# Attention and highway layer on one core: PSUM as eight planned banks, a searched order of issue, and x of the last two duos transposed by DMA

## The chip, the cores and the metric

One NeuronCore of a Trainium2 chip runs the whole program. The metric is the device time in microseconds of one execution, the median of several. The profile's span, from the first to the last instruction, is some 2 us shorter than that time (183.9 against 185.97 for the kernel before).

## The reference

Sliding-window attention with a linear bias (window 128), then a highway layer. Batch 8, 8 heads, 576 positions, head size 64; the layer has 4608 rows of 512.

```python
scores = scale * q @ k.T - slope[h] * |i - j|      # only 0 <= i - j < 128
attn   = softmax(scores); x = attn @ v             # [8, 576, 8 * 64] -> [4608, 512]
H = max(x @ w_h, 0); T = sigmoid(x @ w_t + b_t)
out = T * H + (1 - T) * x
```

## The kernel before

Two batches make a "duo"; duo 0 is cut into stages a, b, c, d, the others into A and B (3B is stage B of duo 3, and its blocks are "3B blocks"). For each stage TensorE (PE) transposes q and k, makes scores, ScalarE (ACT) takes the exponential, VectorE (DVE) multiplies by a mask, PE makes PV, and DVE divides into x. For each block of 128 rows of x, PE transposes x, ScalarE copies it out as xt, and PE computes h (x @ w_h) and z (x @ w_t); this part after the attention is called the FFN. DVE, ScalarE and GpSimd (POOL) combine, and the sync queue (SP) stores. Every instruction belongs to a small piece called a node; a list of nodes gives the order in which all engines' queues are filled. Each engine has a queue of its own, filled in that order.

```python
    psp = ctx.enter_context(tc.tile_pool(name="ps", bufs=BUFS["ps"], space=PSUM))   # bufs 4
    def ps_tile(dt=F32):
        return psp.tile([P, 2, 512 if dt == F32 else 1024], dt, name="ps")          # two banks each
    ...
    def load_v(m, c):                                   # on the gpsimd queue
        n = min(P, S - c * P)
        nc.gpsimd.dma_start(out=VA[m % 2][0:n, c, :, :, 0:D]..., in_=v[...]...)
    def c_ones(i):                                      # column D of each head's slot in v: the row sums
        nc.vector.memset(VA[i][:, :, :, :, D : D + 1], 1.0)
    ...
    def f_xd(m, kind, gi):                              # there, but unused before: DMA_X = ()
        for i in range(n):
            nc.sync.dma_start_transpose(out=xt[:, i], in_=x[:, i, :])
    def f_st(m, kind, gi):                              # four stores a block (two for the short block)
        ...
        for t in range(4):
            nc.sync.dma_start(out=dst[t], in_=ot[32 * t : 32 * t + 32, 0 : len(bs), :])
    ...
    order, end = plan(SHIFT, LOOKS)                     # list scheduling by priorities
    with tc.manual_schedule():
        for t, key in order:
            nodes[key][3]()
```

The softmax here doesn't subtract the row's maximum and nothing guards it: scores larger than these inputs give would overflow.

## Time and profile before

| what | value |
|---|---|
| time, median before the prediction | 185.97 us |
| span of the profile | 183.9 us |
| PE busy | 155.0 us (84%) |
| DVE busy | 141.6 us (77%) |
| last matmul to the end of the span | 6.9 us |

Rows of PE overlap in the profile (four h matmuls are 1.04 us as a row of the timeline and 0.86 us as a piece of the chain of waits), so the pieces of the chain are taken as the price of a group.

### The profile page before, as it was taken

The numbers are of one execution on the slowest core, as the hardware profiler recorded it, in microseconds if no ns is written. First come the engines' busy times: TensorE is split into PE (matmuls) and PEld (weight loads), VectorE is DVE, ScalarE is ACT, GpSimd is POOL, SyncE is SP. The second block draws the span as 40 slices with busy tenths as digits, with TensorE's granted clock in tenths as the row PEclk, the third lists the DMA queues.
The fourth block names the chain that finished last, engine by engine and source line by source line (L and its number), as shares of the span: only waits on it lengthen the run. The fifth ranks groups of instructions, "written<-read, shape, count | busy, mean of one in ns | idle before, by whom it ended". The sixth has DMA issues, their size and how long they took to land.

```text
span 183.9 us, 5244 instructions
## 1 busy us (share of the span) xinstructions
PE 155.0 (84%) x2132; PEld 93.9 (51%) x2132; DVE 141.6 (77%) x253; ACT 127.8 (69%) x178; POOL 121.5 (66%) x132
## 2 busy tenths in 40 slices
PE   0286886779999957997999999999998999999950
PEld 0264655655564524675554565665444666555510
DVE  5339885699999893697688999799899788866770
ACT  2558595753889953879779889786998888445510
POOL 7994123979999945984269953544487787667540
PEclk9999999999999996999999999999999999999995
DMA  4999999999999999999997994142212322243543
GB/s 157 225 187 198 200 199 176 138 132 92 127 207 228 210 200 205 135 187 225 208 135 96 178 159 90 45 103 61 57 45 74 93 66 74 74 103 99 137 128 94
DMA packets 70167, 25.50 MB, mean 139 GB/s; under 512 B 48128, under 2 KB 65024, under 8 KB 70144
## 3 DMA queue, kind: packets, MB, share of 16 engines
q0 software_dynamic: 62832, 14.68, 113.6%
q1 hardware_dynamic: 7312, 10.49, 21.3%
q8 instruction: 16, 0.26, 0.6%
q14 instruction: 7, 0.06, 0.1%
HBM read 30.41 MB, written 9.44 MB: 217 GB/s over the span
## 4 chain that ended last, share of the span: by engine, by line
PE 38%; DMA 26%; DVE 16%; POOL 7%; ACT 5%; issue 3%; SPq 1%; POOLq 0%; DVEq 0%; ACTq 0%
DMA kl<-in_k_dram 24%; PE ps L460 10%; PE ps L443 9%; DVE pt L363 6%; PE ps L386 6%; PE ps L270 5%; PE ps L328 5%; DVE x L403 4%; POOL ot L484 3%; DMA out_dram<-ot 3%; ACT pt L344 2%; PE ps L462 2%; DVE uu L450 2%; POOL ql L110 2%; PE ps L426 2%
## 5 line engine op out<-in xcount | busy, mean ns | idle before, releaser
L344 ACT ACTIVATE pt<-ps,bias 128x1024 bf16<-128x1024 f32 (+1 forms) x80 | 73.4, 951 | 9.1 <-PE ps L328 8.4
L484 POOL TENSOR_TENSOR ot<-uu,x 128x512 f32<-128x512 bf16 x35 | 49.7, 1421 | 30.4 <-DVE uu L478 28.9
L363 DVE TENSOR_TENSOR pt<-pt,mk 128x2048 bf16<-128x2048 bf16 (+1 forms) x40 | 47.8, 1210 | 0.7 <-ACT pt L344 0.5
L460 PE MATMUL ps<-wT,xt 128*128 128x512 bf16 x144 | 38.0, 387 | 1.2 <-DVE uu L450 0.7
L443 PE MATMUL ps<-wH,xt 128*128 128x512 bf16 x144 | 37.2, 380 | 0.6 <-DVE uu L450 0.3
L122 POOL DMA_DIRECT2D va<-in_v_dram x20 | 22.2, 1117 | 14.3 <-DMA kl<-in_k_dram 8.2
L450 DVE SCALAR_TENSOR_TENSOR uu<-ps,x 128x512 bf16<-128x512 f32 x36 | 24.8, 688 | 7.7 <-PE ps L443 7.3
L468 ACT ACTIVATE tt<-ps 128x512 f16<-128x512 f32 x36 | 21.5, 598 | 11.6 <-PE ps L462 11.1
L328 PE MATMUL ps<-qt,kt 64*128 64x256 bf16 (+2 forms) x384 | 27.2, 254 | 1.8 <-DVE kt L295 1.4
L473 POOL TENSOR_SCALAR tt<-tt 128x512 f16<-128x512 f16 x32 | 23.1, 722 | 5.6 <-ACT tt L468 5.5
L435 ACT COPY xt<-ps 128x512 bf16<-128x512 bf16 x36 | 21.0, 586 | 8.1 <-PE ps L426 7.2
L403 DVE TENSOR_TENSOR x<-ps,rd 128x256 bf16<-128x256 f32 (+3 forms) x40 | 25.5, 637 | 1.4
L386 PEld LDWEIGHTS <-pt 128*128 128x128 bf16 (+1 forms) x576 | 21.2, 101 | 8.0 <-issue 1.8
L386 PE MATMUL ps<-va,pt 128*128 128x65 bf16 (+1 forms) x576 | 24.1, 196 | 1.3 <-ACT kt L295 0.4
L295 ACT COPY kt<-ps 128x1024 bf16<-128x1024 bf16 x13 | 13.1, 1012 | 14.4 <-PE ps L270 8.4
L289 DVE COPY qt<-ps 128x1024 bf16<-128x1024 bf16 x16 | 10.9, 687 | 14.2 <-PE ps L270 10.9
L478 DVE TENSOR_TENSOR uu<-uu,tt 128x512 bf16<-128x512 bf16 x36 | 16.6, 462 | 4.9 <-POOL tt L473 2.9
L270 PE MATMUL ps<-ident,ql 128*64 128x128 bf16 (+1 forms) x320 | 13.3, 242 | 8.3 <-DMA ql<-in_q_dram 7.5
L443 PEld LDWEIGHTS <-xt 128*128 128x128 bf16 x144 | 12.1, 97 | 14.4 <-issue 2.8
L460 PEld LDWEIGHTS <-xt 128*128 128x128 bf16 x144 | 12.4, 99 | 13.7 <-issue 3.9
L328 PEld LDWEIGHTS <-kt 64*128 64x128 bf16 x384 | 12.8, 97 | 12.6 <-issue 7.0
L270 PE MATMUL ps<-ident,kl 128*64 128x128 bf16 (+1 forms) x320 | 12.8, 242 | 6.6 <-DMA kl<-in_k_dram 5.6
(46 smaller groups left out, 127.9 us busy)
## 6 DMA issues: line engine op xcount, KB each, us to landing
out_dram<-ot SPq DMA_DIRECT2D x128, 64.0 KB, 1.8
va<-in_v_dram POOLq DMA_DIRECT2D x16, 256.0 KB, 10.8
ql<-in_q_dram POOLq DMA_DIRECT2D x3, 1024.0 KB, 14.6
kl<-in_k_dram POOLq DMA_DIRECT2D x3, 1024.0 KB, 18.8
ql<-in_moe_w_h_dram SPq DMA_DIRECT2D x1, 1024.0 KB, 5.8
out_dram<-ot SPq DMA_DIRECT2D x8, 128.0 KB, 2.4
ql<-in_q_dram POOLq DMA_DIRECT2D x4, 128.0 KB, 5.8
kl<-in_k_dram POOLq DMA_DIRECT2D x4, 128.0 KB, 5.9
```

What stands on the lines that cost most here:

```text
L122: nc.gpsimd.dma_start(out=VA[m % 2][0:n, c, :, :, 0:D].rearrange("s r h d -> s (r h) d"), in_=v[2 * m : 2 * m + 2, :, c * P : c * P + n, : ...
L270: nc.tensor.transpose(out=pt[r * D : (r + 1) * D, c : c + n], in_=L[ps, r, nh * hs + hl, t * D : (t + 1) * D], identity=ident[ps, ps],)
L328: nc.tensor.matmul(out=sc[:, r, o + off : o + off + w_], lhsT=KT[i][rows, h, j * P : (j + 1) * P], rhs=rhs, start=not add, stop=not add or ...
L344: nc.scalar.activation(out=PT[m, home, h // 2][:, h % 2, :, c0 : c0 + W], in_=SC[m, kind, h][:, :, o : o + W], func=ACTF.Exp, bias=BIAS[:, ...
L363: nc.vector.tensor_tensor(out=o, in0=o, in1=mk.to_broadcast([P, 2, rep, W]), op=ALU.mult,)
L386: nc.tensor.matmul(out=av[rows, hl, n * (D + 1) : (n + 1) * (D + 1)], lhsT=pt[:, hl, r, off : off + (D if narrow else P)], rhs=va[:, j, r, ...
L403: nc.vector.tensor_tensor(out=x.rearrange("p b (h d) -> p h b d", h=2), in0=av[:, :, :, 0:D], in1=rd[:, :, 0:nb].to_broadcast([P, 2, nb, D ...
L443: nc.tensor.matmul(out=AH[m, kind, gi][:, i, :], lhsT=XT[m, kind, gi][:, i, c, :], rhs=wH[:, c, :], start=c == 0, stop=c == NCK - 1)
L450: nc.vector.scalar_tensor_tensor(out=uu[:, 0:n, :], in0=AH[m, kind, gi][:, 0:n, :], scalar=0.0, in1=x, op0=ALU.max, op1=ALU.subtract,)
L460: nc.tensor.matmul(out=az, lhsT=XT[m, kind, gi][:, i, c, :], rhs=wT[:, c, :], start=c == 0, stop=False)
L473: eng.tensor_scalar(out=tt, in0=tt, scalar1=0.5, scalar2=0.5, op0=ALU.mult, op1=ALU.add)
L484: eng.tensor_tensor(out=ot[:, 0:n, :], in0=UU.pop((m, kind, gi))[:, 0:n, :], in1=x, op=ALU.add)
```

## The change

Its intent: give each PSUM user only the banks it needs, replace the list scheduler by an order and a bank plan found by a search, and take the x transposes of the last two duos (18 blocks) off PE and ScalarE. The core of the diff (cuts marked "..."):

```diff
-    DMA_X = ()
+    DMA_X = (6, 7, 8, 9)
-    psp = ctx.enter_context(tc.tile_pool(name="ps", bufs=BUFS["ps"], space=PSUM))
+    psp = ctx.enter_context(tc.tile_pool(name="ps", bufs=1, space=PSUM))
+    PSB = psp.tile([P, 8, 512], F32, name="ps")
+    def ps_tile(nb, dt=F32):
+        b = int(next(taken))
+        v = PSB[:, b, :] if nb == 1 else PSB[:, b : b + 2, :]
...
-        pt = ps_tile(BF16)
+        pt = ps_tile(1, BF16)
...
-                    node(("x", kb), "SP", 450 * n, t - 1.3 * dt, lambda kb=kb: f_xd(*kb), alln,
-                         take="xt", uses=[xo], land=1000 * n)
+                    node(("x", kb), "SP", 1250 * n, t - 1.3 * dt, lambda kb=kb: f_xd(*kb), alln,
+                         take="xt", uses=[xo], land=1000 * n, keep="xt")
...
-    order, end = plan(SHIFT, LOOKS)
+    ISSUE = """
+        7 2 0 17 6 8 14 16 11 3 12 5 19 1 18 4 33 24 10 25 34 31 15 20 32 37 28 38 35 21 51 36
...
+        260 203 245 13 252 251 261 248 204 242 195 130 256 92 253 255 125 161 131 154 241 196
...
+    BANKS = """
+        0 1 0 1 2 0 4 6 2 0 6 4 6 2 7 5 7 0 2 3 2 5 7 2 4 1 5 7 3 5 2 3 0 5 6 2 0 1 3 6 0 4 2 1
...
+    order = [names[int(n)] for n in ISSUE.split()]
```

## The prediction

> **What bounds the kernel now.** I read the page first, then the chain of waits in order of time, then TensorE's timeline and the sums by stretch, then the landings of the loads. The page:
>
> ```profile
> PE 155.0 (84%) x2132; PEld 93.9 (51%) x2132; DVE 141.6 (77%) x253; ACT 127.8 (69%) x178; POOL 121.5 (66%) x132
> ...
> PE   0286886779999957997999999999998999999950
> ...
> DMA  4999999999999999999997994142212322243543
> ```
>
> No engine is full over the whole span, but PE is full from about slice 18 on; the DMA engines are full up to about slice 23 (105 us) and idle after. So there are two stages: loads first, PE after. The chain says the same:
>
> ```profile
> 10.27 18.79 DMA kl<-in_k_dram
> 29.10 1.92 PE ps L270 x32
> ...
> 51.27 18.85 DMA kl<-in_k_dram
> 70.16 0.89 PE ps L270 x16
> ...
> 155.11 0.97 PE ps L443 x4
> 156.08 0.22 PE ps L426 x4
> 156.30 0.86 PE ps L460 x4
> 157.38 0.86 PE ps L443 x4
> 158.24 0.73 PE ps L386 x24
> ...
> 178.54 0.68 DVE ot L484
> ```
>
> Two K loads stand on the path: that of duo 1 lands at 29.1 us, that of duo 2 at 70.1 us. From 86 to 162 us the chain is nearly all PE: its pieces give the real price of PE work (rows of the page overlap, so their means are too large). Four h matmuls (L443) cost 0.86 us, an x transpose (L426) 0.22, a 24-matmul PV (L386) 0.73; the h at 155.11, straight after scores, costs 0.97. TensorE's timeline shows what the loads cost:
>
> ```profile
> 29.10 1.92 PE L270 MATMUL ps<-ident,kl 128*64 128x128 bf16 x32 [1.50 <-DMA kl<-in_k_dram]
> ...
> 36.42 0.42 PE L386 MATMUL ps<-va,pt 128*128 128x65 bf16 x8
> ...
> 40.01 1.04 PE L460 MATMUL ps<-wT,xt 128*128 128x512 bf16 x4
> ```
>
> The first PV starts at 36.4 us and the first FFN matmul at 40.0: the gpsimd queue loads q and k of duo 1 (landing by 29.1) before w_t (31.6) and the first v (36.0). Until then PE has only transposes and scores. The sums by stretch show the other engines:
>
> ```profile
> 29.00:70.00 41.00, 34.91 (x499) 21.59 (x499) 34.81 (x68) 28.67 (x40) 33.72 (x34) 1.00 2.83 168
> 70.00:90.00 20.00, 18.65 (x303) 12.38 (x304) 13.79 (x22) 14.93 (x18) 13.84 (x15) 0.91 2.12 188
> 90.00:160.00 70.00, 68.36 (x882) 39.85 (x882) 61.22 (x93) 58.26 (x75) 46.25 (x41) 1.00 0.63 94
> ```
>
> From 90 to 160 us PE is 98% busy and DVE 87%: DVE is the next bound. The last matmul ends at 177.0; u, g, o, the last stores and the end take the other 6.9 of 183.9 us.
>
> [...] h after scores (64-row mode) is 0.97 instead of 0.86, so a switch costs 0.10 us. [...] The old ring gives every user two banks, four buffers in all, though h, z and an x transpose each fill one; PE's table of waits shows single waits of 0.2 to 0.8 us for readers (kt, uu, pt, x), a few us altogether, of which only a part can be for a bank. [...] The 3.1 us wait that ends at 70.1 is followed by a granted clock of 0.83 over 70 to 80, a loss of 1.7 us. [...] No transposing DMA is in this trace; a 64 KB store lands in 1.8 us (median).
>
> **The change part by part.** I decoded both orders of issue from the text (the old from its plan, the new from the numbered list), and priced PE's pieces by the chain.
>
> (1) x of the last two duos by DMA. Removed: 18 transpose groups on PE, 18 x 0.22 = 4.0 us, nearly all inside the PE-bound stage; and 18 ACT copies of 586 ns, 10.5 us, beside other work (ACT has room), worth nothing directly. Added: 18 transposing DMAs of 128 KB on the sync queue. The diff's own table charges 1.25 us of issue each, formerly 0.45, so somebody measured it; 22 us on a queue that mostly waits for POOL. I assume about 2 us more to land.
>
> (2) Mode switches. Counting them along PE's order: 135 before, 118 after; 17 x 0.10 = 1.7 us. Scores, PVs and transposes stand in runs, and z follows its h.
>
> (3) PE work. Summing the pieces, 144.1 us before, 138.4 after: 4.0 + 1.7 less.
>
> (4) Order of the loads. The new queue order is q and k of duo 0, v0, v1, w_t, then q1, v2, k1, v3, k2, v of duo 1, q2. Spacing landings as in the old trace (5.2 us for a q or k of a duo, 2.3 for a v block, 2.5 for w_t, 1 for a tail): first v at 20.9 instead of 36.0, w_t 27.0 instead of 31.6, k1 40.8, k2 52.5 instead of 70.1, q2 63.8. After each landing PE still has a known amount of work, so its end is at least landing plus what is left. Before: k1 29.1 + 131.8 = 160.9; v0 36.4 + 127.9 = 164.3; k2 70.1 + 100.6 = 170.7. Real end 177.0, so 6.3 of slippage in 107 us, 1.7 of it the cold clock. After: v0 20.9 + 130.0 = 150.9; w_t 27.0 + 124.3 = 151.3; k1 40.8 + 113.0 = 153.8; first v of duo 1 58.6 + 97.1 = 155.7; q2 63.8 + 94.1 = 157.9. The binding floor falls from 170.7 to 157.9, by 12.7: 5.7 is less PE work, 7.0 the order.
>
> (5) PSUM by single banks and a full search should cut the short waits; but DVE. From 90 to 160 us PE's work shrinks to about 68.4 - 5 = 63, while DVE's stays 61.2. I take the old slippage without the cold clock, 4.6, and add 1.4 for DVE: 6.0.
>
> (6) The tail. After the last PV the new order has 5.8 us of h and z before the first 3B block; norm 1.1 + issue 1.25 + 2 to land fits. But the last x transpose stands behind two four-part stores (1.7 each): it lands about 15.4 us after the last PV, its h could start at 13.6: a wait of about 1.5 us allowed for. From the last matmul to the end stays 6.9 (the last is z instead of h; tanh and t, 0.9, replace u, 0.7).
>
> (7) The added mask constant falls away: 1.7 us of DVE in the first 10 us, under loads; nothing.
>
> Sum: 157.9 + 6.0 + 1.5 = 165.4 for PE's end, + 6.9 = 172.3 span, + 2.1 (median 185.97 less span 183.9) = 174.4; I say **174 us**, 6.4% less.
>
> **The rivals.** (a) DVE takes over. For: 87% where PE is 98%[...]. Against: its total of 140 us still leaves over 20 us in a 165 us stage, and a searched order knows its costs. It would give 177 to 180. (b) The DMA transposes sit on the path. For: they are issued in order behind stores that wait for POOL; in the new list h of the 3B blocks comes only 1.9 to 4.1 us of PE work after its transpose, of 2A 5 to 9. Against: their DMA traffic is small, with the queues a third full there. If each lands 3 us later than I think, 2B and 3B each lose 2 to 3 us: 178 to 180. (c) The fixed plan is brittle: banks and order come from modelled durations, and a late load holds every in-order engine; v of duo 1 now comes after k2. For: nothing adapts at run time. Against: the old order was fixed too. It would give 180 to 184. (d) It does better than I allow: PE sticks to the floor, 158 + 1 + 6.9 + 2.1 = 168.
>
> **Range and chances.** The centre is 174. Slippage between 2 and 11 us instead of 7.5 gives 169 to 178; (b) and (c) widen the top: 169 to 180. For "within 2%" the time must be over 182.3, that is, 8 of the 12 us must vanish, which needs two rivals at once: 0.06. Slower than 189.7 needs a transpose far costlier than the diff assumes: 0.01. Faster: 0.93.
>
> **What would show it right or wrong.** Right: the first PV near 21 us and FFN matmuls before 30; no PE wait of 3 us for K and a granted clock near 1 from 20 us on; PE ending near 165; mode switches of 0.10 us less often; PE busy about 84% or more, DVE over 80% of the span. Step 1 is wrong if h (L443) waits for xt DMAs by more than 3 us in all, or transposes take over 3.5 us to land. Step 4 is wrong if the first v lands after 25 us or q2 after 68. Step 5 is wrong if between 90 and 150 us PE waits on DVE (uu, x) or sits at 90%. Step 6 is wrong if the end comes over 8 us after PE's last matmul.

## The result, and the profile after

The changed kernel takes **196.18 us** (196.07 to 197.25, 4 runs) against 186.33 for the kernel before on the same chip: 5.5% slower (ratio 1.0548, interval 1.0462 to 1.0633). All ratios here are the mean time of one kernel's fast runs over that of the other's fast runs of the same rounds, so not quite the ratio of the medians quoted. Medians of different occasions differ for the same kernel (the kernel before has 184.86 to 186.59), so a difference across occasions is best read from the ratios; 1 point of ratio (0.01) is about 1.9 us. The prediction of 174 us, range 169 to 180, was wrong.

The page of the changed kernel, whose span is 194.5 us:

```profile
PE 150.3 (77%) x2037; PEld 90.0 (46%) x2060; DVE 146.6 (75%) x244; ACT 116.5 (60%) x160; POOL 118.5 (61%) x132
...
PE   0289789980069899999999999699999999598400
PEld 0267553750046456576655576346455655133100
DVE  6368669750086989998989899988999899329660
ACT  4428657892043799889889689597987711114100
...
PEclk9999999998557999999999999999999999969975
```

PE's row has a hole of two slices (one slice is 4.9 us) at 44 to 53 us, where DVE is empty too and ScalarE nearly, and the clock row falls to 5 in the second of them and in the next. A second weak part stands at the end: 5, 9, 8, 4 instead of a row of nines. The chain of waits (start, length, what) has both:

```profile
20.56 0.40 PE ps L393 x4
...
26.96 1.49 PE ps L449 x3
...
41.20 0.60 DVE uu L456
41.80 12.32 issue
54.20 0.88 DVE qt L290
...
166.04 0.88 PE ps L465 x4
166.92 1.09 SPq L425
168.11 2.46 DMA xt<-x
170.61 1.89 PE ps L449 x4
...
178.76 0.43 SPq L505
179.29 1.20 SPq L425
180.59 0.52 SPq L505
...
185.83 1.72 DMA out_dram<-ot
187.63 0.69 DVE ot L489
```

The first two lines answer to 36.4 and 40.0 us of before: the first PV (L393) at 20.6 and the first FFN matmul (L449) at 27.0. That part of the new order does what it was meant to. Then come 12.3 us of "issue", time in which the engine waited for nothing that the profile could name. At the end SP's own instructions (SPq: L425 a transposing DMA, L505 a store) form the path. The timeline of all engines around the hole, with the idle time before an instruction and its releaser in brackets:

```profile
42.36 0.84 POOL L125 DMA_DIRECT2D va<-in_v_dram  x1
...
54.20 0.87 DVE L290 COPY qt<-ps 128x1024 bf16<-128x1024 bf16 x1 [12.39 <-issue]
54.43 0.12 DVE L183 MEMSET va<- 128x80 bf16 x1
...
54.85 1.15 POOL L125 DMA_DIRECT2D va<-in_v_dram  x1 [11.65 <-DVE va L183]
...
55.12 0.58 PE L329 MATMUL ps<-qt,kt 64*128 64x128 bf16 x11 [11.77 <-DVE qt L290]
55.12 0.42 PEld L329 LDWEIGHTS <-kt 64*128 64x128 bf16 x10 [11.90 <-issue]
...
55.74 0.69 ACT L345 ACTIVATE pt<-ps,bias 128x512 bf16<-128x512 f32 x1 [10.94 <-PE ps L329]
```

DVE comes back at 54.2 us, and next to it stands a memset of va, the ones column, 0.12 us long. The v load issued at 42.36 lands at 54.09 us in the trace: it was issued behind 1 MB of k in the same queue (issued at 41.23, landed at 53.10). The compiled list of DVE's instructions names the wait (no profile; the columns are line, instruction):

```
L456 TensorScalarPtr uu<-ps,x 128x512 [waits PE_49,Activation_49]
L183 Memset va_92 128x80 [waits DMASW4_49]
L290 TensorCopy qt_94<-ps 128x2x512 [waits PE_49,Activation_49]
```

In that list the memset stands before the copy that the profile charges with the wait, and it waits for a DMA: the count of DMASW4_49 that it waits for is the one that this load brings. (In the trace the memset's record starts 0.23 us after the copy's, though it stands before it in the list; why is not known.) The load writes columns 0 to 63 of each head's slot, the memset column 64: they touch no common element, yet the later one is made to wait for the earlier one to the same buffer. The next v load then waits for the memset (11.65), PE for DVE's copy (11.77), ScalarE for PE (10.94). The sums by stretch show the price and its echo in the clock (the columns are stretch, its length, busy time of PE, PEld, DVE, ACT and POOL with instructions in brackets, granted clock, DMA share, GB/s):

```profile
29.00:42.00 13.00, 12.57 (x198) 7.52 (x198) 11.49 (x23) 10.19 (x18) 6.08 (x7) 1.00 1.80 148
42.00:54.00 12.00, 1.35 (x45) 1.13 (x40) 0.00 (x0) 2.80 (x4) 1.20 (x2) 0.72 1.21 121
54.00:70.00 16.00, 14.02 (x175) 8.44 (x177) 13.23 (x27) 9.18 (x13) 11.52 (x12) 0.79 1.30 142
...
160.00:184.00 24.00, 18.80 (x96) 7.76 (x95) 15.42 (x26) 4.76 (x9) 12.11 (x15) 0.93 0.53 125
```

From 42 to 54 us DVE did nothing at all, and the granted clock is 0.72, then 0.79: the trace's clock records have it at half from 47.2 to 60.8 us, so some 6 us of the work after the hole ran at half clock too. From 160 to 184 us PE is busy for only 18.8 of 24.

So there are two suspects: (A) one late memset behind a load, some 12 us; (A2) the sync queue in the last 40 us. The rivals: (B) the DMA transposes as such, with the early hole only taking slack; (C) the fixed plan as such, with new waits of the same size elsewhere when one is removed; and DVE as the bound.

### The profile page after: what moved, and what is told of

It reads as the page before. It is cut to its first block, busy times and chain, and to the rows that moved or that the text cites.

```text
span 194.5 us, 5118 instructions
## 1 busy us (share of the span) xinstructions
PE 150.3 (77%) x2037; PEld 90.0 (46%) x2060; DVE 146.6 (75%) x244; ACT 116.5 (60%) x160; POOL 118.5 (61%) x132
## 4 chain that ended last, share of the span: by engine, by line
PE 44%; DVE 13%; DMA 10%; issue 10%; ACT 9%; SPq 6%; POOL 5%; DVEq 0%; ACTq 0%; POOLq 0%
PE ps L465 12%; PE ps L449 10%; PE ps L393 7%; PE ps L329 7%; ACT pt L345 6%; DMA va<-in_v_dram 6%; DVE pt L364 5%; SPq L505 4%; DVE x L410 4%; PE ps L271 4%; DMA out_dram<-ot 3%; PE ps L467 2%; POOL kl L113 2%; POOL ql L113 2%; PE ps L433 2%
## 5 line engine op out<-in xcount | busy, mean ns | idle before, releaser
L345 ACT ACTIVATE pt<-ps,bias 128x1024 bf16<-128x1024 f32 (+1 forms) x80 | 71.3, 946 | 26.6 <-PE ps L329 26.2
L489 POOL TENSOR_TENSOR ot<-uu,x 128x512 f32<-128x512 bf16 x35 | 44.0, 1259 | 23.1 <-DVE uu L483 12.6
L449 PE MATMUL ps<-wH,xt 128*128 128x512 bf16 x130 | 36.9, 401 | 7.8 <-DMA xt<-x 4.8
L478 POOL TENSOR_SCALAR tt<-tt 128x512 f16<-128x512 f16 x32 | 25.7, 810 | 23.1 <-ACT tt L473 23.0
L329 PE MATMUL ps<-qt,kt 64*128 64x256 bf16 (+2 forms) x384 | 25.5, 250 | 12.6 <-DVE qt L290 12.0
L483 DVE TENSOR_TENSOR uu<-uu,tt 128x512 bf16<-128x512 bf16 x36 | 23.3, 666 | 6.6 <-POOL tt L478 6.2
L393 PEld LDWEIGHTS <-pt 128*128 128x128 bf16 (+1 forms) x576 | 21.9, 103 | 12.2 <-issue 5.3
L393 PE MATMUL ps<-va,pt 128*128 128x65 bf16 (+1 forms) x576 | 25.3, 199 | 2.8 <-DMA va<-in_v_dram 1.0
L329 PEld LDWEIGHTS <-kt 64*128 64x128 bf16 x384 | 13.8, 97 | 23.6 <-issue 20.0
L449 PEld LDWEIGHTS <-xt 128*128 128x128 bf16 x144 | 12.8, 101 | 21.7 <-DMA xt<-x 6.6
L290 DVE COPY qt<-ps 128x1024 bf16<-128x1024 bf16 x16 | 10.9, 694 | 14.9 <-issue 12.4
L465 PEld LDWEIGHTS <-xt 128*128 128x128 bf16 x144 | 13.1, 100 | 15.7 <-issue 3.3
L271 PE MATMUL ps<-ident,kl 128*64 128x128 bf16 (+1 forms) x320 | 12.4, 233 | 8.6 <-DMA kl<-in_k_dram 8.6
L271 PEld LDWEIGHTS <-kl 128*64 128x64 bf16 (+1 forms) x320 | 10.1, 129 | 9.9 <-DMA kl<-in_k_dram 9.4
L467 PE MATMUL ps<-bT,ones 128*128 128x512 bf16 x36 | 13.6, 379 | 0.0
## 6 DMA issues: line engine op xcount, KB each, us to landing
ql<-in_q_dram POOLq DMA_DIRECT2D x3, 1024.0 KB, 12.4
```

The source lines that it names most:

```text
L271: nc.tensor.transpose(out=pt[r * D : (r + 1) * D, c : c + n], in_=L[ps, r, nh * hs + hl, t * D : (t + 1) * D], identity=ident[ps, ps],)
L329: nc.tensor.matmul(out=sc[:, r, o + off : o + off + w_], lhsT=KT[i][rows, h, j * P : (j + 1) * P], rhs=rhs, start=not add, stop=not add or ...
L345: nc.scalar.activation(out=PT[m, home, h // 2][:, h % 2, :, c0 : c0 + W], in_=SC[m, kind, h][:, :, o : o + W], func=ACTF.Exp, bias=BIAS[:, ...
L393: nc.tensor.matmul(out=av[rows, hl, n * (D + 1) : (n + 1) * (D + 1)], lhsT=pt[:, hl, r, off : off + (D if narrow else P)], rhs=va[:, j, r, ...
L449: nc.tensor.matmul(out=AH[m, kind, gi], lhsT=XT[m, kind, gi][:, i, c, :], rhs=wH[:, c, :], start=c == 0, stop=c == NCK - 1)
L465: nc.tensor.matmul(out=az, lhsT=XT[m, kind, gi][:, i, c, :], rhs=wT[:, c, :], start=c == 0, stop=False)
```

## The experiments

Twelve kernels ran, all correct. The ratio in each line is that to the kernel before of the same rounds.

| run | edit | median us | ratio | interval |
|---|---|---|---|---|
| the change | | 196.18 | 1.0548 | 1.046 to 1.063 |
| k1_ones_first | memset early | 185.75 | 1.0031 | 0.994 to 1.012 |
| k11_swap | memset just before the load | 186.22 | 1.0076 | 0.997 to 1.018 |
| k2_before_ones_late | before, memset late | 192.06 | 1.0419 | 1.031 to 1.053 |
| k12_split_only | stores on two queues | 187.87 | 1.0212 | 1.011 to 1.031 |
| k7_ones_split_st | k1 and the split | 180.45 | 0.9601 | 0.948 to 0.972 |
| k9_split_deferred | k7, mended | 179.14 | 0.9713 | 0.964 to 0.979 |
| k6_ones_first_x67 | k1, DMA x in one duo | 183.18 | 0.9857 | 0.976 to 0.995 |
| k4_ones_first_pe_x | k1, no DMA x | 185.96 | 1.0060 | 0.998 to 1.014 |
| k8_pe_x_split_st | k4 and the split | 184.33 | 0.9894 | 0.981 to 0.998 |
| k10_pe_x_deferred | k9, no DMA x | 186.79 | 1.0157 | 1.011 to 1.020 |
| k3_before_dma_x | before, DMA x alone | 192.17 | 1.0284 | 1.016 to 1.040 |
| k5_old_order_banks | old order, banks alone | 182.99 | 0.9836 | 0.972 to 0.996 |

One caution on k5 to k8, which shared their rounds. Five of the seven runs of the kernel before are listed as slow there (over 1.5% above the fastest, 183.26 us). The ratios come out as if four of the seven, with a mean of 186.02, had been taken; against the two fast (183.26 and 184.39) k5 is 0.995, k6 0.997, k7 0.972 and k8 1.001. How these four compare with each other does not depend on it.

### The memset: k1, k11, k2

k1 moves entry 13 to the front; k11 only swaps it with the load one place ahead of it; k2 does the reverse to the kernel before.

```diff
 k1
-        7 2 0 17 6 8 14 16 11 3 ...
+        7 2 0 17 6 8 13 14 16 11 3 ...
-        260 203 245 13 252 ...
+        260 203 245 252 ...
 k11
-        260 203 245 13 252 ...
+        260 203 13 245 252 ...
 k2 (kernel before, after its plan)
+    order.remove(("ones", 1))
+    order.insert(order.index(("v", 1, 4)) + 1, ("ones", 1))
```

> The changed kernel with one entry of its order moved: the memset of the ones column of the second v buffer goes back to the start, before any v load of duo 1. Theory A (this memset, issued after a v load into the same buffer, waits for that load's landing and blocks DVE, then PE, ACT and GpSimd from 41.8 to 54.2 us; TensorE's clock halves after it): the 12.4 us wait is gone, the granted clock stays near 1, and the time falls from 196.2 to 178 to 184 us. Rival B (the transposing DMAs and the sync queue they fill set the end, the early stall is only absorbed slack): the time stays above 190 us. Rival C (brittle fixed banks): new waits of the same size appear elsewhere, above 188 us.

> The changed kernel with two neighbours of its order swapped: the late memset of the ones column and the load of the last v block of duo 1, which stands one place ahead of it, change places; the memset stays at its late place on DVE. Theory A (it is only the wait for that load, not the late place, that costs): the 12.4 us wait is gone and the time is that of k1_ones_first, 184 to 188 us. Rival (the late place on DVE or a full DVE costs): it stays above 192 us.

> The kernel before with the same memset moved the other way: right behind the issue of the last v load of duo 1 (issued at 46.3, landed at 57.8 us in its trace). Theory A: DVE stands still for about 10 us until that load lands, and the time rises from 186 to 192 to 198 us. Rivals B and C: the position of one memset of 0.13 us is worth under 2%, 184 to 189 us.

Measured: 185.75, 186.22 and 192.06 us. k1 misses its stated range of 178 to 184 by 1.75 us, but the fall of 10.4 us (5.2 points of the ratio, 9.6 us) is most of the wait, and rival B's 190 and rival C's 188 are not reached. The stretch of the hole, in the changed kernel and then in k1:

```profile
29.00:70.00 41.00, 27.94 (x410) 17.09 (x411) 24.72 (x50) 22.17 (x34) 18.80 (x20) 0.83 1.43 138
```

```profile
29.00:70.00 41.00, 35.42 (x565) 22.57 (x566) 34.53 (x63) 31.60 (x46) 27.83 (x30) 0.96 2.00 172
```

k11 and k2 lie inside their ranges for theory A (184 to 188 and 192 to 198). In k11 the memset is at the same late place on DVE and the cost is gone as well; the compiled list shows it without a wait. So what cost time is the wait for that one load, not the late place. In k2, DVE's timeline has the hole in the old kernel too, here put down to the load (in the compiled list the memset, which waits for all five v loads of the duo, stands just before this reciprocal):

```profile
56.73 0.36 DVE L402 RECIPROCAL rd<-ps 128x4 f32<-128x4 f32 x1 [10.73 <-DMA va<-in_v_dram]
56.96 0.12 DVE L180 MEMSET va<- 128x80 bf16 x1
```

A 10.7 us hole, and 4.2% more time (7.8 us on 185.0). Theory A holds: one memset of 0.12 us behind one load is worth some 10 of the 22 us by which the prediction missed.

### The sync queue: k12 and k7

k12 is the change, k7 is k1, both with every second store of the last 13 blocks on ScalarE's queue:

```diff
+        late = m == 3 or (m == 2 and kind == "B" and gi > 0)
+        q_ = lambda n: nc.scalar if late and n % 2 else nc.sync
-            nc.sync.dma_start(out=dst[t], in_=ot[...])
+            q_(t).dma_start(out=dst[t], in_=ot[...])
```

> The changed kernel with the memset left late and only the last stores split over two queues. It tells whether the two causes add: if they do, 196.2 less the 4 to 7 us that the split gave on top of the early memset, 188 to 192 us. If the stall early on hides the backlog or the other way round, 194 to 197 us.

> k1_ones_first (memset early, DMA transposes kept), with every second store of the last 13 blocks issued from ScalarE's queue instead of the sync queue. In k1 the sync queue is busy without a gap from 141 to 181 us: x of 3B0 is issued 5 us after it is ready, PE waits 6.4 us for xt and the last store goes out 6 us after PE's end. Theory A2 (the sync queue is the bound of the last 40 us: 1.2 us per transpose and 1.85 us per block of stores against 2 us of PE work per block): xt waits fall under 2 us, the end comes 8 us after PE's last matmul, and the time falls from 185.8 to 174 to 179 us. Rival: DVE or the fixed banks hold the end, and it stays above 183 us; or the stores hold ScalarE up and it gets slower.

k1's timeline of the sync queue shows why (start, length, what, count; the stretch is read as one queue in order):

```profile
149.41 7.12 SPq L505 DMA_DIRECT2D out_dram<-ot  x12
156.64 2.51 SPq L425 DMA_TRANSPOSE xt<-x  x2
159.24 1.94 SPq L505 DMA_DIRECT2D out_dram<-ot  x4
161.28 1.19 SPq L425 DMA_TRANSPOSE xt<-x  x1
162.57 1.18 SPq L497 DMA_DIRECT2D out_dram<-ot  x2
163.84 1.25 SPq L425 DMA_TRANSPOSE xt<-x  x1
165.18 3.83 SPq L505 DMA_DIRECT2D out_dram<-ot  x8
169.11 1.20 SPq L425 DMA_TRANSPOSE xt<-x  x1
170.41 9.47 SPq L505 DMA_DIRECT2D out_dram<-ot  x20
```

A record of this queue contains its own wait: in the first line one store took 1.8 us instead of 0.4. From 156.6 to 180 us no store took over 0.6 us, and no gap is over 0.11 us. A store in four parts takes 1.9 us of the queue and a transpose 1.2, so a block of the last duo needs 3.1 us of it while PE needs about 2 (h 0.86, z 0.86 and its bias 0.22 in the chain). The x of the first 3B blocks is issued at 156.6, though the last norm ended at about 151.8; and the last 20 stores leave from 170.4 us on, while PE's last matmul ends at 175.4. (My expectation for k7 said "busy without a gap from 141 to 181"; from 141 to 181 the queue's own waits add up to 5.4 us, nearly all before 150.) PE's table of waits, the changed kernel, k1 and then k7 (total, times, longest, in us):

```profile
PE ps L449 <- DMA xt<-x: 4.8, 2, 2.6
```

```profile
PE ps L449 <- DMA xt<-x: 6.4, 4, 3.1
```

```profile
PE ps L449 <- ACT tt L473: 2.3, 1, 2.3
PE ps L449 <- DVE uu L456: 1.8, 1, 1.8
...
PE ps L449 <- DMA xt<-x: 0.4, 1, 0.4
```

The waits for xt are nearly gone in k7, and k12's table has none for xt at all. k12 falls by 3.4 points of the ratio, 6.2 us (8.3 us between the medians of two occasions), to just under the 188 to 192 expected, while its memset wait stays:

```profile
DVE qt L290 <- issue: 11.8, 1, 11.8
```

The two causes add: 5.2 points for the memset (k1), 3.4 for the queue (k12), 8.6 together; both at once (k7) take away 9.5, or 8.3 by the caution above. Two of k7's four runs were slow, the profiled one among them; its ratio rests on two fast runs, 178.41 and 178.77, which lie inside the 174 to 179 I gave (the median, 180.45, does not).

### What the DMA transposes are worth: k4, k8, k6, k3

k4 takes the DMA transposes out of k1, k8 out of k7, k6 out of k1's last duo only; PE transposes come back about 1.5 us of PE work before their use, with banks given anew (least recently used). k3 puts them alone into the kernel before, by its old plan.

```diff
 k4, k8 (and k6: (6, 7))
-    DMA_X = (6, 7, 8, 9)
+    DMA_X = ()            # and ISSUE, BANKS written anew
 k3 (kernel before)
-    DMA_X = ()
+    DMA_X = (6, 7, 8, 9)
-                    node(("x", kb), "SP", 450 * n, ...
+                    node(("x", kb), "SP", 1250 * n, ...
```

> As k1_ones_first, but x of all duos is transposed by TensorE and copied by ScalarE as before; the new order is kept, each such pair put about 1.5 us of PE work before its first use; banks then given anew, least recently used first. Theory A with the sync queue as second cause: waits for xt (4.8 us) and the backlog of stores at the end go, PE has 4 us more to do: equal to k1 or up to 4 us faster, 175 to 181 us. If the DMA transposes are a gain by themselves, it is 3 to 5 us slower than k1.

> k4_ones_first_pe_x (no DMA transposes, memset early) with the same split of the last stores over two queues. Theory A2: the stores alone (1.85 us per block) are below PE's 2.2 us per block, so the queue is no bound without transposes; the split gives 0 to 4 us, 181 to 186 us. If it lands with k7 at 174 to 179, the transposes by DMA were worth nothing and the queue of stores was all.

> k1_ones_first with the DMA transposes kept for the third duo (stages 6 and 7) and taken away for the last one (9 groups back on PE and ScalarE); banks given anew. Theory A2: the sync queue has 9 x 1.25 = 11 us less to issue where it is the bound, PE 2 us more: 178 to 183 us, xt waits for DMA under 1 us. Rival: no change, 184 to 188 us.

> The kernel before with one part of the change alone: x of the last two duos transposed by DMA on the sync queue, order by the old plan (with 1.25 us per transpose in it), PSUM as before. Theory A: this part alone costs or wins little; PE saves 4 us, the sync queue (1.2 us per transpose, 1.85 us per block of stores) delays the last blocks by 3 to 5 us: 182 to 190 us. Rival B: it alone makes the kernel slower by about the 10 us seen, 193 to 199 us.

With one queue, k1 and k4 are equal (1.003 and 1.006): what PE and ScalarE gain is given back at the sync queue. (k4's 185.96 us is above the 175 to 181 I gave, though "equal to k1" came true.) With the stores split, in the same rounds, k7 against k8 is 0.960 against 0.989: the transposes by DMA are then worth 2.9 points, about 5.5 us, where I had put 4.0. Part of that can be k8's order, in which the pairs were put back by rule and not by a new search; no run tells this apart. k8's 184.33 us lies inside its 181 to 186. Half of the transposes with one queue (k6) is 183.18 us, just above the 178 to 183 expected, with 1.7 us of waits for xt where I had put under 1; whether it is better than k1 is not told across the two occasions (0.986 or 0.997 against 1.003). In the old order the transposes cost 2.8% (k3: two fast runs, 189.7 and 190.7 us, at the top of the 182 to 190 I gave).

### The banks alone: k5

The old order, x by TensorE, eight single banks, least recently used first (and without the mask constant).

> The order of the kernel before with PSUM as eight single banks (least recently used first) and x by TensorE: the bank part of the change alone, without the mask constant. If the ring of four double buffers held TensorE up, 180 to 184 us; if not (waits on readers were under 0.8 us each), as before within 2%, 183 to 189 us.

182.99 us, 1.6% faster (interval 0.972 to 0.996), or 0.5% by the caution above. It lies inside the first of my ranges (180 to 184) and at the edge of the second (183 to 189), and under the 2% I would call a clear difference: the banks are no cause of the loss, and that they help is not shown.

### A mended version: k9, and k10

In k7 a store at the head of ScalarE's queue held up a tanh, and PE behind it (the 2.3 us above). k9 sends ScalarE's half of each store two blocks later and makes the output tile six single buffers instead of three double ones; k10 is the same without DMA transposes.

```diff
-    ... "tt": 3, "ot": 3,
+    ... "tt": 3, "ot": 6,
-        ot = op.tile([P, 2, DM], F32, name="ot")
+        ot = op.tile([P, 1, DM], F32, name="ot")
+        while HELD and (end or HELD[0][0] <= len(SEEN) - LAGST):     # LAGST = 2
+            o_, i_ = HELD.pop(0)[1:]
+            nc.scalar.dma_start(out=o_, in_=i_)
```

> k7_ones_split_st mended where its trace shows a new wait (a store at the head of ScalarE's queue held a tanh, and so PE, up for 2.3 and 1.8 us after the last PV): ScalarE's half of each store is issued two blocks later, and the output tile has six single buffers instead of three double ones, the same bytes. Theory A2 (with the early memset wait and the sync queue's backlog out of the way, the sum of the prediction holds): PE ends at 166 to 170 us, the time is 173 to 178 us, 4 to 7% under before. Rival: DVE, at 90% from 70 to 150 us, is the bound, and it stays at 178 to 182 us.

> The same mending without any transpose by DMA (x by TensorE and ScalarE for all duos). It tells what the DMA transposes are worth once the queue is no bound: PE has 18 x 0.22 = 4 us more. Expected 3 to 5 us above k9, 177 to 182 us; equal to k9 if ScalarE, DVE or the tail set the end.

k9: 179.14 us, 2.9% under the kernel before, with five of six runs fast; above the 173 to 178 expected, and inside the 178 to 182 of the rival there, DVE as the bound, which no run took apart (PE's end, 167.7, is inside the 166 to 170 expected). Whether it is better than k7 is not told: they ran on different occasions, k7 with two fast runs only. Both beat both kernels of this study; k9's interval, 0.964 to 0.979, does not clear 2%, so the record calls it unclear. k10 missed its range upward: 186.79, slower even than k8. Its trace shows a new wait of 2.6 us of a tanh behind a store that waited for an earlier store, so it is no clean measure of the transposes; k7 against k8 is a cleaner one.

What is left in k9 between its 177.3 us of span and the 172.3 of the prediction's sum: q of duo 2 lands at 64.5 (63.8 predicted), PE ends at 167.7 (165.4), and 9.6 us follow PE's last matmul (6.9). In the stretch that was 98% PE and 87% DVE before, it now reads:

```profile
90.00:150.00 60.00, 57.35 (x754) 33.36 (x762) 56.55 (x82) 45.94 (x57) 42.69 (x39) 1.00 1.09 143
```

DVE is busy for 94% of the time, PE for 96%. That the rest of the slippage is DVE's is argued from this line, not shown by a run.

## Why the prediction was wrong

**Step 4, the order of the loads, is the step that failed.** (In this paragraph k1 and k2 with a landing time are the keys of duos 1 and 2, not runs.) It took "the new queue order" as moving loads only. Its landings were right: first v 20.5 us (20.9 predicted), w_t 25.2 (27.0), k1 39.7 (40.8), k2 53.1 (52.5); q2 came at 65.1 in k1 (63.8) but at 70.5 in the changed kernel, because the stall held its issue back. What it left out is that the same list moves other writers against the loads. I had decoded the memset's place, one behind the load, and not asked what it must wait for. (In the kernel's own list of nodes neither the memset nor the load names the other; only PV names both. The search is not in the file.) DVE stood for 12.4 us; that is some 10 us of the time (k1), which no term of the sum and neither (a), (b) nor (c) of the rivals named, although (c) had the form of it: a late load that holds in-order engines (here DVE for 12.4 us, PE for 11.8, ScalarE for 10.9).

**Steps 1 and 6, the sync queue, were mis-sized.** I called it "a queue that mostly waits for POOL" and allowed 1.5 us of wait for the last transpose. The queue's issue time was right (1.2 us against 1.25, 1.9 a block of stores against 1.7), and 3.1 us a block against PE's 2 could have been worked out from those two numbers; I summed it for the last transpose only and not for the whole stage. Measured: 4.8 us of waits for xt in the changed kernel and 6.4 in k1, where step 1 had called over 3 a sign of being wrong; 10.6 us from PE's last matmul to the end in the changed kernel instead of 6.9; and 6 to 8 us of time (k12). Rival (b) had the mechanism, at 178 to 180 us in all, since it saw only the latency, not the queue's rate.

**What was right.** The saving of the transposes (4.0 us predicted, about 5.5 measured with the queue out of the way, the order of k8 aside). The landing, in the main: 1.25 and about 2 us were assumed, and 14 of the 18 landed 2.4 to 3.1 us after the start of their issue; but three beside the v loads at 122 to 130 us took 5.6 to 7.2 and one 3.6, over the 3.5 that step 1 had set as its limit. DVE's share: 87% became 94%; that it is the next bound is not shown. The clock: in the changed kernel PE's 11.8 us wait ended at 55.1 us, and the granted clock was 0.72 from 42 to 54 us and 0.79 from 54 to 70 (half from 47.2 to 60.8). In k1 it was 0.96 from 29 to 70 us and 0.67 from 170 to 185: its clock records have half clock only for 3.4 us after the 2.5 us wait for q of duo 2 and from 171.6 us on, when PE was nearly done. The banks: small at most. The fewer mode switches, step 2, were not tried by themselves: their 0.10 us each is my estimate from the chain of the kernel before (four h matmuls 0.97 us after scores, 0.86 after z), and what makes up that difference is not shown.

**The account.** 5.2 points for the memset and 3.4 for the queue are 16 us, which would leave 180 of 196.2. Measured with both mended together: 177 to 180 us (fast runs of k7 and k9), 3 to 6 above the 174. In k9's trace the rest is 0.7 us in the floor (q2's landing), 1.6 in the slippage (PE's end is 9.1 us after the floor instead of 7.5) and 2.7 in the tail. That these are sizes only is argued, not tried.

## What to carry to other kernels

A search over the order of issue is only as good as the dependences it knows: after it, go through the compiled list for waits that no edge of its model stands for, above all small memsets and constants that share a buffer with a DMA. Treat a DMA queue as an engine: add up its issue time per block and set it against the slowest engine's time per block before moving work onto it. When a change bundles parts, undo each alone; here two faults, of some 10 and of 6 to 8 us, hid a version that is about 3% faster than before.
